# Fused attention and soft mixture of experts: score units of 384 and 2x192 queries, turns in 64-row pieces, another order of tasks

## The chip, the cores and the metric

The kernel runs on one core of one Trainium2 chip. The metric is the device time of one execution in microseconds (us); lower is better. Engines are named as in the profile: PE is TensorE (matmuls), PEld its weight loads, DVE is VectorE, ACT is ScalarE, POOL is GpSimd, SP issues most DMAs.

## The reference: what is computed

The first half is attention over 8 batches of 8 heads, 576 positions by 64 dimensions, in float32. Queries and keys are rotated, the scores are scaled by 1/8, softmax runs over the keys, and the result is multiplied with the values. The second half is a soft mixture of experts over the 4608 tokens of 512 features that come out: logits with 32 slots, a softmax over the tokens (to fill the slots) and one over the slots (to read them back), and between them 8 experts with two layers of weights.

```python
scores = scale * np.matmul(q_rot, k_rot.transpose(0, 1, 3, 2))
scores = scores - np.max(scores, axis=-1, keepdims=True)
attn = np.exp(scores)
attn = attn / (np.sum(attn, axis=-1, keepdims=True) + 1e-09)
return np.matmul(attn, v).astype(np.float32)
```

## The kernel before

Two heads form a pair; there are 32 pairs, and four pairs (one batch) form an image. One head of a pair lies in SBUF rows 0 to 63 and the other in rows 64 to 127. The rotated values are split into a float16 high part and a float16 rest, so a score is a sum of four products: high by high, high by rest, rest by high, and a fourth one that adds the negated maximum (a row of `peak` times a constant in `lift`).

Work on a pair is cut into named tasks:

- `load0/1`, `spin0/1`, `join`, `high0/1`, `low` bring queries and keys in and rotate and split them. `spin` is POOL's, in eight instructions a pair; `join` and `low` are DVE's, `high` is ACT's.
- `m00` to `m31` (`m_unit`, L232 to L237) find the maxima. Four blocks of 128 queries each meet two halves of 288 keys. A unit is two matmuls (one a head, in the two row halves of the array) into a PSUM slot, and one DVE maximum over it. `m_rem` does the last 64 queries; `m_min`, `m_turn`, `m_half`, `m_rows` join the maxima, turn them on PE and send them into `peak`.
- `t0` to `t7` (`t_unit`, L271 to L297) make the exponentials: four key blocks of 128 by two halves of 288 queries. A unit is eight matmuls and one ACT exponential from PSUM into `a_t`. `t8` does the last 64 keys.
- `av0` to `av7` (`av`, L313) multiply with the values: 18 float32 matmuls each, in two column halves of 64. `av8` does the last 64 keys. `av` 2i and 2i+1 use key block i for the two heads.
- `o_out`, `o_down`, `recip`, `norm`, `natural`, `natural_out`, `logits`, `logits_sum` divide by the sum, turn the result (`natural`, five transposes, L367) and form the logits.
- Once an image: `stat`, `slots` and `soft` tasks for the two softmaxes (L393 to L456).

The array is used in several forms of tile, told here as rows by columns: scores and maxima 64x128, the remainders (`t8`, `m_rem`, `av8`) 64x64, `av` 128x64, turns 128x128, `logits` and `slots` 128x32.

All results of matmuls but those of `av` go through three PSUM slots of two banks each, taken in turn (`bank2`, L223); the next use of a slot waits until DVE or ACT has read it.

The order in which each engine meets its tasks is written out by hand: `WHEN` gives each task a due time by pair (modulo 4), `FIRST` that of pairs 0 to 4. The line of all tasks is sorted by due time plus 4 a pair, and each engine, SP and POOL included, works in that order. Tasks of `stat`, `slots` and `soft` do something for every fourth pair only. After the loop follow the last pair, the slots, the two expert layers and the output, with weights that stream in as buffers come free.

Of the kernel before, what the change touches and what calls it, by code (L numbers as in the profile page):

```python
# [7 lines left out]
F32 = mybir.dt.float32  # L8
# [36 lines left out]
N_SLOT = 0  # L45
# [4 lines left out]
N_A = 4  # L50
# [56 lines left out]
    "o_out": (-7.38923, 1.30837, 3.82693, 4.15198, 4.48727), "o_down": (-7.29683, 1.10071, 3.8762, 4.38997, 4.1384),  # L107
    "load1": (-0.7099, -14.46932, -27.91086, -20.43743, -23.33867), "trickle0": 0.4431, "trickle1": 1.2621,
    "trickle2": 2.5296, "trickle3": 3.4658, "recip": (3.8412, 1.95047, 6.75772, 4.80839, 5.05393),
    "high0": (7.26462, -27.61978, -21.33278, -16.62529, -12.03782),  # L110
    "spin1": (7.79554, -28.94545, -24.54925, -20.2484, -19.67269), "norm": (8.00273, 5.36418, 8.13811, 5.60813, 6.09061),
    "load0": (8.7347, -28.06246, -28.81748, -28.24952, -23.67445),
    "natural": (10.20728, 6.24301, 8.6185, 6.45263, 7.72938), "stat0": 10.27075,
    "natural_out": (10.54469, 7.30376, 8.92233, 6.67229, 7.90351),
    "logits": (10.65333, 7.57842, 9.53379, 7.51041, 10.2191),
    "logits_sum": (11.0822, 7.58469, 9.67175, 7.84223, 10.75836), "stat1": 11.4484, "soft0": 11.65971, "soft1": 11.88823,
    "slots": 12.01632, "soft2": 13.55606, "soft3": 14.76066,
    "high1": (19.50237, -27.97373, -20.95698, -15.76925, -12.86183),
    "load_v": (19.88526, -18.22242, -5.34305, -5.07004, -2.7109),
# [5 lines left out]
def attn_softmoe(ctx, tc, qk, v, phi, w, cs, ident, sel, seg, out):  # L125
# [142 lines left out]
    ats = {}  # L268
    rems = {}

    def t_unit(p, u):  # L271
        i, n = divmod(u, 2)
        hl, pk, s = halves[p], peaks[p % 2], bank2()
        for w, (k, q) in enumerate(((KH, QH), (KH, QL), (KL, QH), (None, None))):
            first, last = w == 0, w == 3
            for h in range(2):
                lhs = lift[rows[h]] if k is None else hl[rows[h], k]
                rhs = pk[rows[h]] if k is None else hl[rows[h], q]
                if u < KB - 1:
                    if k is not None:  # L280
                        lhs = lhs[:, P * i:P * i + P]
# [11 lines left out]
        else:  # L293
            if n == 0:
                ats[p, i] = att.tile([P, 2, S], F32, name="a_t", bufs=N_A)
# [614 lines left out]
```

## Time and profile before

| | us |
|---|---|
| median of 3 runs | 532.02 |
| lowest, highest | 531.54, 532.99 |
| span of the profiled execution | 531.8 |
| PE busy | 503.4 (95%) |
| DVE, ACT, POOL busy | 359.4, 309.4, 250.5 |

The profiled execution is one of its own; its span, from the first instruction to the last, is what the stretches below add up to. The page gives busy time by engine, the span in 40 slices, and the groups of instructions by line; the trace answers by stretch and instruction. A matmul's end is modelled, so the distance from one group's start to the next group's start is the better measure of what a group costs PE.

### The profile page before, as it was taken

What the parts mean: (1) busy time and instruction counts of PE and PEld (TensorE: products, weight loads), DVE (VectorE), ACT (ScalarE), POOL (GpSimd) and SP (SyncE); (2) the same over time, 40 slices, a digit from 0 to 9 for tenths busy, and PEclk for the clock granted to TensorE, in tenths of its full rate; (3) what the DMA queues carried; (4) which work ended last, traced back from release to release, by engine and by line L of the source; (5) the groups of instructions that cost most, each with busy time, mean ns of one, the idle gap of its engine ahead of it and who ended that gap; (6) DMA issues with size and microseconds to landing.
All of it is one profiled execution on the core that took longest, in us unless ns stands there. A gap on an engine that the chain in (4) does not pass through costs nothing.

```text
span 531.8 us, 24105 instructions
## 1 busy us (share of the span) xinstructions
PE 503.4 (95%) x10836; PEld 385.8 (73%) x10836; DVE 359.4 (68%) x577; ACT 309.4 (58%) x621; POOL 250.5 (47%) x330
## 2 busy tenths in 40 slices
PE   3799999999999999999999999999999999989991
PEld 2377788878787778787877787778777887853661
DVE  5989867777777777677767776777777762143162
ACT  2156575766675666666666666666666665563352
POOL 3956976636545554655555555555445211210000
PEclk9699999999999999999999999999999999999997
DMA  7244433546441644154425443544345171379998
GB/s 252 95 155 162 162 118 116 197 144 224 140 159 51 215 154 163 48 204 158 161 103 196 157 156 116 193 161 157 116 138 215 38 291 60 134 282 383 394 364 330
DMA packets 28487, 93.92 MB, mean 177 GB/s; under 512 B 4064, under 2 KB 5856, under 8 KB 28384
## 3 DMA queue, kind: packets, MB, share of 16 engines
q1 hardware_dynamic: 28370, 92.37, 48.3%
q8 instruction: 85, 1.39, 1.0%
q14 instruction: 18, 0.15, 0.1%
q10 hardware_dynamic: 14, 0.00, 0.0%
HBM read 82.85 MB, written 9.44 MB: 174 GB/s over the span
## 4 chain that ended last, share of the span: by engine, by line
PE 86%; DVE 6%; ACT 4%; issue 1%; DMA 1%; SPq 0%; DVEq 0%; ACTq 0%
PE o_ps L317 26%; PE s_ps L282 24%; PE s_ps L235 8%; PE o_ps L324 4%; PE s_ps L367 3%; PE a_ps L789 3%; PE a_ps L769 3%; PE s_ps L286 2%; DVE nm L237 2%; PE s_ps L379 2%; PE t_ps L815 2%; PE s_ps L431 1%; PE s_ps L288 1%; PE s_ps L243 1%; DMA x_in<-in_qk 1%
## 5 line engine op out<-in xcount | busy, mean ns | idle before, releaser
L237 DVE TENSOR_REDUCE nm<-s_ps 128x2 f32<-128x576 f32 x256 | 184.9, 754 | 64.0 <-PE s_ps L235 61.9
L200 POOL TENSOR_TENSOR x_in<-x_in,cs_sb 128x288 f32<-128x288 f32 x248 | 197.4, 832 | 55.7 <-DMA x_in<-in_qk 54.2
L297 ACT ACTIVATE a_t<-s_ps 128x576 f32<-128x576 f32 x256 | 150.8, 656 | 117.6 <-PE s_ps L282 116.8
L317 PEld LDWEIGHTS o_ps<-v_in,a_t 128*64 128x64 f32 x4608 | 145.3, 138 | 28.0 <-issue 25.6
L317 PE MATMUL o_ps<-v_in,a_t 128*64 128x65 f32 x4608 | 163.1, 225 | 0.0
L282 PE MATMUL s_ps<-hl 64*128 64x288 f16 x1536 | 135.2, 284 | 0.4 <-DVE nm L237 0.2
L351 POOL TENSOR_TENSOR xn<-o_sb,rr 128x512 f32<-128x512 f32 x31 | 33.4, 1078 | 143.2 <-ACT a_t L297 78.2
L282 PEld LDWEIGHTS <-hl 64*128 64x128 f16 x1536 | 74.6, 94 | 22.8 <-issue 3.0
L282 PE MATMUL s_ps<-peak,lift 64*128 64x288 f16 x512 | 74.9, 283 | 0.0
L235 PE MATMUL s_ps<-hl 64*128 64x288 f16 x512 | 63.6, 290 | 4.9 <-DVE nm L237 2.7
L209 ACT CAST hl<-x_in 128x576 f16<-128x576 f32 (+1 forms) x66 | 41.0, 658 | 17.8 <-DVE x_in L204 17.8
L213 DVE TENSOR_TENSOR hl<-x_in,hl 128x1152 f16<-128x1152 f32 x32 | 45.7, 1429 | 0.5 <-ACT hl L209 0.5
L204 DVE TENSOR_TENSOR x_in<-x_in 128x1152 f32<-128x1152 f32 (+1 forms) x35 | 44.7, 1278 | 0.8 <-POOL x_in L200 0.7
L235 PEld LDWEIGHTS <-hl 64*128 64x128 f16 x512 | 24.7, 96 | 20.1 <-issue 6.6
L245 DVE TENSOR_REDUCE nm<-s_ps 128x2 f32<-128x576 f32 x32 | 24.3, 758 | 16.8 <-PE s_ps L243 16.8
L373 ACT COPY xt<-s_ps 128x576 f32<-128x576 f32 x32 | 20.3, 634 | 17.9 <-PE s_ps L367 17.6
L282 PEld LDWEIGHTS <-lift 64*128 64x128 f16 x512 | 26.6, 94 | 5.5 <-issue 0.5
L324 PE MATMUL o_ps<-v_in,a_rem 64*64 64x65 f32 x1152 | 30.5, 223 | 0.0
L367 PE MATMUL s_ps<-id_sb,xn 128*128 128x128 f32 (+1 forms) x160 | 26.0, 274 | 1.2 <-DVE xn L351 1.2
L324 PEld LDWEIGHTS o_ps<-v_in,a_rem 64*64 64x64 f32 x1152 | 26.4, 133 | 0.5 <-issue 0.2
L297 ACT ACTIVATE a_rem<-s_ps 128x640 f32<-128x640 f32 x32 | 22.6, 705 | 7.0 <-PE s_ps L288 6.6
L367 PEld LDWEIGHTS s_ps<-id_sb,xn 128*128 128x128 f32 (+1 forms) x160 | 19.0, 140 | 7.5 <-issue 7.0
(162 smaller groups left out, 502.0 us busy)
## 6 DMA issues: line engine op xcount, KB each, us to landing
x_in<-in_qk SPq DMA_DIRECT2D x62, 576.0 KB
w_exp<-in_w SPq DMA_DIRECT2D x64, 512.0 KB
v_in<-in_v SPq DMA_DIRECT2D x32, 325.0 KB
out<-w_exp SPq DMA_DIRECT2D x18, 512.0 KB
x_in<-in_qk SPq DMA_DIRECT2D x4, 288.0 KB
cs_sb<-in_cs SPq DMA_DIRECT2D x2, 288.0 KB
peak<-mr SPq DMA_DIRECT2D x31, 2.0 KB
peak<-mr SPq DMA_DIRECT2D x31, 0.2 KB
```

The costliest lines, as they stand in the source:

```text
L200: eng.tensor_tensor(out=x[:, :, c], in0=x[:, :, c], in1=cs_sb[:, :, c], op=ALU.mult)
L204: nc.vector.tensor_tensor(out=x[:, t, 0, c], in0=x[:, t, 0, c], in1=x[:, t, 1, c], op=ALU.add)
L209: nc.scalar.copy(out=halves[p][:, 1 + t, c], in_=loaded[p][:, t, 0, c])
L213: nc.vector.tensor_tensor(out=hl[:, 0:4:3], in0=x[:, :, 0], in1=hl[:, 1:3], op=ALU.subtract)
L235: nc.tensor.matmul(s[:, h, 0:HC], lhsT=hl[rows[h], QH, P * j:P * j + P], rhs=hl[rows[h], KH, half[n]], start=True, stop=True)
L237: nc.vector.tensor_reduce(out=maxima(p)[:, n, j:8:4], in_=s[:, :, 0:HC], axis=AX.X, op=ALU.max, negate=True)
L282: nc.tensor.matmul(s[:, h, 0:HC], lhsT=lhs, rhs=rhs[:, half[n]], start=first, stop=last)
L297: nc.scalar.activation(out=a, in_=s, func=AF.Exp, scale=SCALE)
L317: nc.tensor.matmul(o, lhsT=ats[p, i][:, h, D * t:D * t + D], rhs=vts[p][:, u], start=(i == 0 and j == 0), stop=False)
L324: nc.tensor.matmul(o, lhsT=rems[p][r, at:at + D], rhs=vts[p][r, KB - 1 + h], start=False, stop=(j == (4 if c == h else 3)))
L351: eng.tensor_tensor(out=x[:, 0:4].rearrange("p j h d -> p h j d"), in0=o[:, 1:9, 0:D].rearrange("p (h j) d -> p h j d", h=2), in1=rr[:, 1: ...
L367: nc.tensor.transpose(t[:, P * j:min(P * j + P, S)], xns[p][r, j], id_sb[r, r])
```

## The change

Units. `UNITS` names six units a pair, `x0`, `x1`, `y0`, `x2`, `x3`, `y1`. An x unit takes one 128-row block by 384 columns; a y unit takes two blocks by the remaining 192 columns each. This holds for the maxima (`mx`, `my`: blocks of queries by keys) and for the exponentials (`tx`, `ty`: blocks of keys by queries). Each unit is read by one instruction of 128 x 768 elements in place of 128 x 576. `a_t` becomes two tiles of two key blocks in place of four tiles of one, so `av` 0 to 3 read from `tx0`, `tx1`, `ty0` and `av` 4 to 7 from `tx2`, `tx3`, `ty1`.

Turns. `m_turn`, `natural`, the turns of `slots` and those of `soft` use `turn64`: the 64 upper and the 64 lower rows are transposed apart, each with 64 columns of the identity, into different PSUM banks. `natural` becomes nine pieces in place of five transposes, `m_turn` two in place of one, `stat1` four in place of two, `soft0` three in place of two. What reads them is rearranged to suit.

Order. All due times are new. The last `av` task of a pair in the line, whichever it is, closes the accumulation (`closing`, `ends`).

```diff
-N_SLOT = 0
+N_SLOT = 2
-N_A = 4
+N_A = 2
+XC, YC = 384, 192
+UNITS = ("x0", "x1", "y0", "x2", "x3", "y1")
...
-    def m_unit(p, j, n):
-        hl, s = halves[p], bank2()
-        for h in range(2):
-            nc.tensor.matmul(s[:, h, 0:HC], lhsT=hl[rows[h], QH, P * j:P * j + P], rhs=hl[rows[h], KH, half[n]],
-                             start=True, stop=True)
-        nc.vector.tensor_reduce(out=maxima(p)[:, n, j:8:4], in_=s[:, :, 0:HC], axis=AX.X, op=ALU.max, negate=True)
+    def spans(u):
+        g, k = divmod(u, 3)
+        if k < 2:
+            return g, [(2 * g + k, slice(0, XC), slice(0, XC))]
+        return g, [(2 * g + i, slice(XC, S), slice(YC * i, YC * i + YC)) for i in range(2)]
+
+    def m_unit(p, u):
+        hl, s, (g, ps) = halves[p], bank2(), spans(u)
+        for j, cols, at in ps:
+            for h in range(2):
+                nc.tensor.matmul(s[:, h, at], lhsT=hl[rows[h], QH, P * j:P * j + P], rhs=hl[rows[h], KH, cols],
+                                 start=True, stop=True)
+        o, i, j = maxima(p), s[:, :, 0:XC], ps[0][0]
+        o = o[:, 0, j:8:4] if len(ps) == 1 else o[:, 1, 0:8].rearrange("p (h j) -> p h j", h=2)[:, :, j:j + 2]
+        i = i if len(ps) == 1 else i.rearrange("p h (j x) -> p h j x", j=2)
+        nc.vector.tensor_reduce(out=o, in_=i, axis=AX.X, op=ALU.max, negate=True)
...
+    def turn64(o, i, h):
+        nc.tensor.transpose(o, i[rows[h]], id_sb[rows[h], rows[h]])
+
     def m_turn(p):
         flat[p] = t = bank2()
-        nc.tensor.transpose(t[0:9, 0, 0:P], nms.pop(p), id_sb)
+        nm = nms.pop(p)
+        for h in range(2):
+            turn64(t[0:9, h, 0:D], nm, h)
...
+    PRODUCTS = ((KH, QH), (KH, QL), (KL, QH), (None, None))
+
     def t_unit(p, u):
-        i, n = divmod(u, 2)
+        hl, pk, s, (g, ps) = halves[p], peaks[p % 2], bank2(), spans(u)
+        for w, (k, q) in enumerate(PRODUCTS):
+            for j, cols, at in ps:
+                for h in range(2):
+                    lhs = lift[rows[h]] if k is None else hl[rows[h], k, P * j:P * j + P]
+                    rhs = pk[rows[h], cols] if k is None else hl[rows[h], q, cols]
+                    nc.tensor.matmul(s[:, h, at], lhsT=lhs, rhs=rhs, start=(w == 0 and at.start == 0), stop=(w == 3),
+                                     skip_group_check=True)
+        if (p, g) not in ats:
+            ats[p, g] = att.tile([P, 2, 2, S], F32, name="a_t", bufs=N_A)
...
     def natural(p):
         flat["n", p] = t = bank2().rearrange("p n x -> p (n x)")
         for j in range(NJ):
-            r = slice(0, P) if j < 4 else rows[1]
-            nc.tensor.transpose(t[:, P * j:min(P * j + P, S)], xns[p][r, j], id_sb[r, r])
+            for h in range(j // 4, 2):
+                at = 256 * (h + 1) + D * j
+                turn64(t[:, at:at + D], xns[p][:, j], h)
...
     def slot_tasks(b):
-        nc.tensor.transpose(t[:, 0, 0:P], dt[:, 0:P], id_sb)
-        nc.tensor.transpose(t[:, 0, P:2 * P], dt[:, D:192], id_sb)
+        for c in range(2):
+            for h in range(2):
+                turn64(t[:, h, D * c:D * c + D], dt[:, D * c:D * c + P], h)
...
     def c_soft_tasks(b, tp=None):
-        tp = bank2()[:, 0] if tp is None else tp
+        if tp is None:
+            tp = bank2().rearrange("p n x -> p (n x)")[:, 448:]
+            turn64(tp[:, 0:D], lb[:, 0:P], 0)
+            turn64(tp[:, D:P], lb[:, 0:P], 1)
+            turn64(tp[:, P:P + D], lb[:, D:192], 1)
```

The due times, sorted, give PE this line of tasks for a pair in the steady part (here from `av0` of pair 17 to the next `av0`; the number behind the dot is the pair, and a bar stands where the form of the tiles changes):

```
before: av0.17 av1.17 | m00.19 m21.19 m10.19 | av2.17 av3.17 | t6.17 t7.17 m30.19 | av4.17 av5.17 |
        m_turn.18 natural.16 | m11.19 m20.19 | av6.17 av7.17 | logits.16 | m01.20 t0.18 |
        t8.18 m_rem.19 av8.17 | m31.19 t1.18 t2.18 t3.18 t4.18 t5.18 |
after:  av0.17 av1.17 | m_turn.18 mx1.19 mx0.19 | av5.17 av2.17 av4.17 | mx3.19 natural.15 my1.19 |
        av7.17 av3.17 av6.17 | logits.15 | m_rem.19 t8.18 av8.17 |
        mx2.19 tx1.18 tx0.18 ty0.18 ty1.18 tx2.18 tx3.18 my1.20 |
```

Pairs that close an image have `slots` and `soft` beside it: before, `slots` stands between `m01` and `t0` and the turns of `stat1` and `soft0` beside `m_turn`; after, the line is `logits`, then `stat1`, `tx0`, `soft0` (64x128), then `slots`, then the remainders. Counted over the 32 pairs of the loop, groups of one form follow each other 409 times before and 273 times after: up to `av0.5` 77 and 43, from there to `av0.30` 313 and 211, and behind it 19 and 19. The order of SP, POOL, DVE and ACT is sorted from the same line.

## Rows read from the trace of the kernel before

**Rows 1.** The page, busy time of each engine, share of the span, instructions.

```profile
PE 503.4 (95%) x10836; PEld 385.8 (73%) x10836; DVE 359.4 (68%) x577; ACT 309.4 (58%) x621; POOL 250.5 (47%) x330
```

**Rows 2.** The page, the chain that ended last, shares by engine.

```profile
PE 86%; DVE 6%; ACT 4%; issue 1%; DMA 1%; SPq 0%; DVEq 0%; ACTq 0%
```

**Rows 3.** Stretches: length, busy us by engine, granted clock, DMA share, GB/s.

```profile
28.60:98.80 70.20, 69.21 (x1565) 54.59 (x1563) 56.03 (x76) 43.30 (x80) 49.55 (x56) 1.00 0.43 150
98.80:445.40 346.60, 345.31 (x8056) 274.62 (x8054) 254.85 (x407) 220.65 (x449) 177.44 (x236) 1.00 0.44 153
475.00:531.80 56.80, 45.03 (x494) 25.27 (x494) 19.22 (x34) 22.61 (x47) 1.74 (x2) 0.95 0.94 370
```

**Rows 4.** PE in time order, one pair: start us, length us, line, matmul, count.

```profile
248.53 0.30 PE L235 MATMUL s_ps<-hl 64*128 64x288 f16 x2
...
251.38 1.27 PE L317 MATMUL o_ps<-v_in,a_t 128*64 128x65 f32 x36
252.58 0.54 PE L235 MATMUL s_ps<-hl 64*128 64x288 f16 x6
...
254.25 0.54 PE L282 MATMUL s_ps<-hl 64*128 64x288 f16 x6
...
255.24 0.29 PE L235 MATMUL s_ps<-hl 64*128 64x288 f16 x2
255.46 1.27 PE L317 MATMUL o_ps<-v_in,a_t 128*64 128x65 f32 x36
256.66 0.28 PE L256 MATMUL s_ps<-id_sb,nm 128*9 128x128 f32 x1
...
257.31 0.51 PE L235 MATMUL s_ps<-hl 64*128 64x288 f16 x4
...
258.95 0.43 PE L379 MATMUL s_ps<-xt,phi_sb 128*32 128x128 f32 x8
...
259.50 0.30 PE L235 MATMUL s_ps<-hl 64*128 64x288 f16 x2
...
260.22 0.32 PE L286 MATMUL s_ps<-hl 64*64 64x320 f16 x1
...
261.71 0.29 PE L235 MATMUL s_ps<-hl 64*128 64x288 f16 x2
```

**Rows 5.** PE in time order, the tasks of an image, pair 17 to 18.

```profile
269.84 0.33 PE L419 MATMUL s_ps<-id_sb,d_t 128*128 128x128 f32 x1
...
271.11 0.46 PE L235 MATMUL s_ps<-hl 64*128 64x288 f16 x4
...
272.69 0.43 PE L379 MATMUL s_ps<-xt,phi_sb 128*32 128x128 f32 x8
...
273.16 0.30 PE L235 MATMUL s_ps<-hl 64*128 64x288 f16 x2
273.39 0.42 PE L427 MATMUL s_ps<-xn,dn 64*32 64x128 f32 x8
...
274.75 0.54 PE L282 MATMUL s_ps<-hl 64*128 64x288 f16 x6
```

**Rows 6.** Waits over the whole span: us in total, times, longest.

```profile
PEld o_ps L317 <- issue: 25.6, 108, 0.2
```

**Rows 7.** The chain in order of time: start us, us, what.

```profile
36.16 1.77 PE o_ps L317 x54
```

**Rows 8.** ACT in time order, behind `av8` of the pair of Rows 4.

```profile
249.31 0.21 ACT L341 COPY o_sb<-o_ps 64x65 f32<-64x65 f32 x1
249.54 2.82 ACT L297 ACTIVATE a_t<-s_ps 128x576 f32<-128x576 f32 x5
```

**Rows 9.** DVE in time order, three maxima in a row.

```profile
252.92 2.09 DVE L237 TENSOR_REDUCE nm<-s_ps 128x2 f32<-128x576 f32 x3 [0.63 <-PE s_ps L235]
```

**Rows 10.** Groups by line: busy us, mean ns of one, idle before.

```profile
L317 PEld LDWEIGHTS o_ps<-v_in,a_t 128*64 128x64 f32 x4608 | 145.3, 138 | 28.0 <-issue 25.6
L282 PEld LDWEIGHTS <-hl 64*128 64x128 f16 x1536 | 74.6, 94 | 22.8 <-issue 3.0
```

More of the change, by code (lines that the diff above doesn't have):

```diff
@@ L76 @@
-    "natural": (6.70186, 6.65236, 6.60514, 6.72707), "natural_out": (6.79597, 6.82414, 6.78729, 6.79597),
-    "logits": (7.35988, 7.35988, 7.32871, 7.35629), "logits_sum": (7.55748, 7.56266, 7.52049, 7.57479), "stat0": 8.99027,
-    "stat1": 10.08425, "slots": 11.94902, "soft0": 14.63727, "soft1": 15.70384, "soft2": 16.5487, "soft3": 17.5679,
[8 rows of a table added]
+    "m_min": (-9.24898, -10.07141, -10.65543, -9.67809), "m_turn": (-8.98144, -8.69694, -9.73808, -8.79403),
+    "m_half": (-8.33553, -8.69136, -9.6611, -8.52608), "m_rows": (-7.75001, -7.7324, -7.20975, -8.49008),
[8 rows of a table added]
@@ L79 @@
+    "o_out": (-2.97471, -2.27101, -1.8983, -2.04174), "o_down": (-2.76277, -2.66479, -1.62675, -1.921),
+    "trickle0": 0.4431, "recip": (0.5462, -1.59196, 0.70867, -1.5243), "trickle1": 1.2621,
+    "norm": (1.40693, 2.40265, 2.01973, -0.5723), "weights": (1.52098, 2.94306, 5.30645, 2.79672), "trickle2": 2.5296,
+    "trickle3": 3.4658, "natural": (3.77628, 4.75891, 3.62412, 2.82399),
+    "natural_out": (4.0295, 4.82885, 3.80343, 3.47442), "logits": (4.23692, 5.31816, 4.15935, 3.75073),
[4 rows of a table added]
 }
 FIRST = {
-    "low": (-29.80024, -21.29316, -19.54716, -14.41668, -8.44168),
@@ L108 @@
[L108 to L119, printed above, removed]
+    "soft1": (-106.26016, 16.43236, 10.79557, 11.72811, 7.16191),
@@ new lines @@
+    "my1": (-44.6697, -35.03551, -11.91368, -11.5224, -11.25324),
+    "stat1": (-44.19886, -8.00974, 12.04812, 8.28776, -8.88907),
+    "m_min": (-41.06115, -18.77578, -10.99567, -9.70908, -10.07557),
+    "m_turn": (-39.52861, -15.90387, -8.55189, -9.44574, -9.22444),
+    "m_half": (-29.77836, -15.43198, -8.46718, -8.88665, -8.78896),
+    "m_rows": (-27.94385, -10.69285, -8.32528, -8.59172, -7.86257),
+    "spin0": (-25.18684, -128.90538, -45.55858, -39.20673, -23.3854),
+    "load1": (-24.78219, 0.95005, -3.43378, -39.46747, -25.60339),
@@ new lines @@
+    "tx1": (-24.77367, -7.50828, -6.43911, -7.08093, -5.47045),
+    "t8": (-24.6024, -8.78392, -6.63374, -6.18281, -6.43356),
+    "ty0": (-18.79426, -7.11206, -6.36065, -7.03321, -5.97768),
+    "tx0": (-16.58157, -7.57331, -6.55964, -7.09157, -7.42017),
+    "tx3": (-16.56176, -5.38841, -5.89139, -7.17421, -5.20658),
+    "tx2": (-16.04543, -6.97169, -6.09068, -6.86208, -5.36696),
+    "ty1": (-15.72052, -7.18171, -6.45846, -5.49631, -5.24744),
+    "av0": (-14.0397, -5.03411, -5.63536, -5.11218, -5.0999),
@@ new lines @@
+    "norm": (2.50123, 3.29159, 1.88404, 2.41613, 3.43322), "natural": (2.51048, 3.69668, 3.59742, 2.66055, 3.91089),
+    "trickle2": 2.5296, "natural_out": (3.06016, 4.35405, 3.69233, 3.059, 3.91405),
+    "soft3": (3.24866, 13.93403, -1.18617, 15.43812, -58.85051), "trickle3": 3.4658,
+    "logits": (5.88191, 5.17781, 3.85488, 4.05922, 5.24522),
+    "logits_sum": (6.69807, 5.1858, 4.23867, 4.29405, 5.39864),
+    "high1": (6.80455, -43.55573, -29.59167, -20.40784, -15.69632),
+    "join": (8.39752, -56.14516, -33.18771, -25.40403, -18.6904),
@@ L120 @@
+    "slots": (12.08535, 4.68036, -1.9515, 9.51451, -23.44866),
+    "stat0": (12.87256, -17.45215, -4.13504, 6.88734, 5.35013),
+    "high0": (21.45985, -48.47894, -28.72707, -22.32542, -16.74733),
 }
@@ L269, in attn_softmoe, with t_rem @@
     rems = {}
+    PRODUCTS = ((KH, QH), (KH, QL), (KL, QH), (None, None))
     def t_unit(p, u):
-        i, n = divmod(u, 2)
+        hl, pk, s, (g, ps) = halves[p], peaks[p % 2], bank2(), spans(u)
[8 more added lines that the diff above has]
+            ats[p, g] = att.tile([P, 2, 2, S], F32, name="a_t", bufs=N_A)
+        a, s = ats[p, g], s[:, :, 0:XC]
+        if len(ps) == 1:
+            a = a[:, ps[0][0] % 2, :, 0:XC]
+        else:
+            a, s = a[:, :, :, XC:S].rearrange("p j h x -> p h j x"), s.rearrange("p h (j x) -> p h j x", j=2)
+        nc.scalar.activation(out=a, in_=s, func=AF.Exp, scale=SCALE)
+    def t_rem(p):
         hl, pk, s = halves[p], peaks[p % 2], bank2()
-        for w, (k, q) in enumerate(((KH, QH), (KH, QL), (KL, QH), (None, None))):
+        for w, (k, q) in enumerate(PRODUCTS):
             first, last = w == 0, w == 3
             for h in range(2):
-                lhs = lift[rows[h]] if k is None else hl[rows[h], k]
+                lhs = lift[rows[h], 0:D] if k is None else hl[rows[h], k, 512:S]
                 rhs = pk[rows[h]] if k is None else hl[rows[h], q]
-                if u < KB - 1:
-                    if k is not None:
-                        lhs = lhs[:, P * i:P * i + P]
-                    nc.tensor.matmul(s[:, h, 0:HC], lhsT=lhs, rhs=rhs[:, half[n]], start=first, stop=last)
-                    continue
-                lhs = lhs[:, 0:D] if k is None else lhs[:, 512:S]
                 rhs = rhs.rearrange("p (j x) -> p j x", x=D)
@@ L289, in t_unit @@
                                  skip_group_check=True)
[L290 to L297 removed]
+        rems[p] = a = att.tile([P, 10 * D], F32, name="a_rem", bufs=2)
+        nc.scalar.activation(out=a, in_=s.rearrange("p n x -> p (n x)")[:, 192:832], func=AF.Exp, scale=SCALE)
     o_ps = ps_o.tile([P, 2, 512], F32, name="o_ps")
@@ L311, in cell, with ends @@
         return c, j, o_flat[rows[c], at:at + VC]
+    closing = {}
+    def ends(p, h, c, j, u):
+        return closing[p, h] == u and j == (4 if c == h else 3)
     def av(p, u):
@@ L316, in av @@
             c, j, o = cell(h, t)
-            nc.tensor.matmul(o, lhsT=ats[p, i][:, h, D * t:D * t + D], rhs=vts[p][:, u], start=(i == 0 and j == 0), stop=False)
+            nc.tensor.matmul(o, lhsT=ats[p, i // 2][:, i % 2, h, D * t:D * t + D], rhs=vts[p][:, u], start=(i == 0 and j == 0),
+                             stop=ends(p, h, c, j, u))
     def av_rem(p):
@@ L324, in av_rem @@
                 nc.tensor.matmul(o, lhsT=rems[p][r, at:at + D], rhs=vts[p][r, KB - 1 + h],
-                                 start=False, stop=(j == (4 if c == h else 3)))
+                                 start=False, stop=ends(p, h, c, j, KB - 1))
     def blocks(t):
@@ L597, in attn_softmoe @@
     }
-    for j in range(4):
-        for n in range(2):
-            plan[f"m{j}{n}"] = lambda p, j=j, n=n: m_unit(p, j, n)
+    for u, n in enumerate(UNITS):
+        plan[f"m{n}"] = lambda p, u=u: m_unit(p, u)
+        plan[f"t{n}"] = lambda p, u=u: t_unit(p, u)
+    plan["t8"] = t_rem
     for b in range(KB):
-        plan[f"t{b}"] = lambda p, b=b: t_unit(p, b)
         plan[f"av{b}"] = (lambda p, b=b: av(p, b)) if b < KB - 1 else av_rem
@@ L615, in attn_softmoe @@
     line = sorted((at(name, p), name, p) for name in WHEN for p in range(NPAIR))
+    for _, name, p in line:
+        if name[:2] == "av":
+            u = int(name[2:])
+            closing.update({(p, h): u for h in range(2) if u == KB - 1 or u % 2 == h})
     load(0)
@@ L648, in attn_softmoe @@
             release_io()
-        if held and "wx" in hold and all((f"t{b}", NPAIR - held) in done for b in range(KB)):
+        if held and "wx" in hold and all((f"t{n}", NPAIR - held) in done for n in UNITS + ("8",)):
             held -= 1
```

66 lines of the change are left out of this document (33 added, 33 removed), and 44 rows, old and new, of tables (FIRST, WHEN).

## The prediction

> **What bounds the kernel now.** I read the page's busy times first. TensorE is busy for 95% of the span and no other engine for more than 68% [rows 1]. Then the chain of waits: 86% of what sets the end is PE, 1% DMA [rows 2]. Then the stretches. From 28.6 us to 475 us PE has hardly a gap (345.3 of 346.6 us in the long stretch) at a granted clock of 1.00, with DMA at 0.44 [rows 3]; only the end, 475 to 531.8, is full of DMA (0.94), and no line of it belongs to this change. So the question is what PE spends inside one pair. The 25 pairs between 98.8 and 445.4 take 346.60 / 25 = 13.86 us each [rows 3].
>
> A pair without image work runs from 248.53 to 261.71, 13.18 us [rows 4]. From start to start, in us: scores and maxima 2.85 (248.53 to 251.38), 0.47 (252.58 to 254.25 less an `av` group of 1.20), 1.21 (254.25 to 255.46), 0.44 (257.31 to 258.95 less 1.20), 0.72 (259.50 to 260.22), together 5.69; four `av` groups of 1.20 each, 4.80; the turns 0.65 (256.66 to 257.31); logits 0.55; remainders 1.49.
>
> Two prices are hidden in these. Sixteen score matmuls of 288 columns take 0.99 us (254.25 to 255.24), two side by side, so 0.124 a couple; the next couple, the last before an `av` group, takes 0.22 (255.24 to 255.46). Leaving the score form thus costs 0.10; three couples in 0.47 say the same (0.37 + 0.10). An `av` group of 36 takes 1.20 and one of 54 takes 1.77 [rows 7], so 18 matmuls are 0.57 and a group has 0.05 on top. The waits confirm it: 108 times the first weight load behind a score group stood idle for some 0.24 us with nothing to release it [rows 6]. Forty couples stream in 40 x 0.124 = 4.96; with five exits (0.50) that is 5.46 of the 5.69, and 0.23 are waits, most of it in the run of five `t` units, which is 2.85 instead of 21 x 0.124 + 0.10 = 2.70.
>
> **The change part by part, a pair without image work.**
>
> *Columns.* Four x units of 384 and two y units of 2 x 192 are 2304 columns, as eight of 288 were, in as many matmuls. The stream stays at 4.96. [...]
>
> *Order.* The sorted line has three score groups a pair in place of five: exits 0.30 for 0.50. `av` goes as 36 + 54 + 54: 1.20 + 1.77 + 1.77 = 4.74 for 4.80. The remainders follow `logits` directly and stay at 1.49. `logits` waits for nothing late, so it takes the 0.47 that it takes in the image pair (272.69 to 273.16) [rows 5] in place of 0.55.
>
> *Turns.* Five transposes and one of the maxima make 0.65 now, a group of their own. No row shows a 64-row piece. Bounds: a turn of 128 columns takes about 0.11 (0.65 for five full ones, a last one of 64, and the way out); a piece has 64 columns, so 0.055. If the two halves run side by side, as the two matmuls of every score couple do, six couples are 0.33; if they follow each other, eleven pieces are 0.60. Both ends are saved the group of their own. I take 0.33, since score couples are the same form of tile.
>
> *Waits.* All six `t` units now stand in one run between maxima, so each meets ACT. Five exponentials of 576 follow each other every (2.82 - 0.65) / 4 = 0.54 us, 0.65 being the length of one [rows 8]; 768 elements are at most 0.72 in proportion. PE makes a `t` unit in 4 x 0.165 = 0.66. ACT is free about 1.0 after the score group began (249.54 against 248.53), then ends exponential k at 1.0 + 0.72 k. PE, with a maximum of 0.17 in front, starts unit k + 1 at 0.17 + 0.66 k. Three slots and the maximum make unit 4 wait for exponential 1 (1.72 against 2.15), 5 for 2 (2.44 against 2.81), 6 for 3 (3.16 against 3.47), and the closing maximum for 4 (3.88 against 4.13). ACT gives way each time, by 0.25 at the least. What is late next is that closing maximum, if a cast stands in ACT's queue inside the run; in the sorted line `high0` and `high1` stand behind it. DVE: three maxima in 2.09 are 0.67 apart [rows 9], so at most 0.89 for 768; six of these replace eight of 0.67, 5.3 for 5.4 a pair, no relief and no new load. The last exponential is done at 5.3, when PE ends `av0`, `av1` (4.30 + 0.10 + 1.20 = 5.6); the next maxima take its slot. So the 0.23 of waits goes; because I followed only one pair's queues, I put 0.10 back.
>
> *Sum.* 4.96 + 0.30 + 0.33 + 4.74 + 0.47 + 1.49 = 12.29 for 13.18: 0.89 saved, 0.79 with the 0.10.
>
> *Image work.* It adds (13.86 - 13.18) x 4 = 2.7 an image. Two turns beside `m_turn` make that group 1.27 (269.84 to 271.11) for 0.65; `slots` costs 0.23 + 1.36 (273.16 to 274.75) and splits a score group; `soft` turns do the rest [rows 5]. After: 1.36, one exit of 0.10, four couples of pieces at 0.055, and 0.2 of what I can't place: 1.9. Saved 0.8 an image, 0.20 a pair.
>
> *Whole.* 25 pairs x (0.79 + 0.20) = 24.8. Before 98.8 the groups fall from 77 to 43: 34 x 0.075 (the mean of 0.10 and 0.05) = 2.5, and seven turn groups gain 1; PE is full there from 28.6 on [rows 3], so this counts, while the first 28.6 us hang on DVE's maxima, whose sum is unchanged. Say 3, between 0 and 6, for I can't follow all first waits of POOL and SP. The pairs behind 445.4 keep 19 groups, but their turns get shorter: 1. Together 28.8: 531.8 - 28.8 = 503.0. The median of the runs lies 0.2 above this span, which I leave out. SP's and POOL's queues pass loads and `norm` in another order; POOL is busy 47% and hides this, and one pair's chain of load, `spin` and `join` would have to be late by more than the 0.25 above to be seen.
>
> [...]
>
> **The rivals.**
>
> 1. *The weight load paces short couples.* A load of 64x128 float16 lasts 94 ns, one of float32 138 [rows 10]. If a half of the array held each load that long, the 20 couples of 192 (16 in `ty`, 4 in `my`) would cost 0.011 more each, and six turn couples 0.083 more: 0.72 a pair, x 32 = 23, so 526. Against: `av` starts two matmuls every 0.064 (1.15 / 18) with loads of 138, so a load's length is mostly latency.
> 2. *The same mechanism, slower than before.* If the two halves' loads also follow each other, a couple of 192 takes 0.188, 0.105 more: 20 x 0.105 = 2.1 a pair, 67 in all: 503 + 67 = 570. It decides for slower from 0.045 a couple on (0.89 / 20), that is, from 0.128. For it: no score couple here is shorter than 0.124. Against: the quadrants of the remainders start six loads and matmuls within 0.13 (260.22 on), and `av` as above.
> 3. *Turn pieces follow each other.* 0.60 for 0.33, 0.27 a pair, 9 in all, with the images 1.5: 513. For: the pieces are float32 where scores are float16. Against: `av` is float32 and runs two halves at once.
> 4. *The run of `t` is ACT's.* If casts (0.67 each) or a late `o_out` fall into it, each pair gives back 0.3 to 0.6: 512 to 522. For: ACT waits 0.25 at the least, so one cast is too much. Against: the sorted line.
> 5. *No waits at all*, and a start 6 shorter: 531.8 - 25 x 1.09 - 6 - 1 = 497.5.
>
> **How the numbers follow.** The forecast 0.60 (own range 499 to 508), rival 1 0.06, rival 2 0.05, rival 3 0.12, rival 4 0.08, rival 5 0.09. About 0.3% is what can be told from no change here. Faster: all but rival 2 and a tail of rivals 1 and 4, 0.93; the same 0.02; slower 0.05. The range 495 to 517 leaves out rivals 1 and 2 and half of 4, and the far end of 5.
>
> **What would show it.** A pair of 12.2 to 12.5 us in the long stretch; 18 matmuls of `av` unchanged; a couple of 192 columns about 0.083 apart; the pieces of `natural` done in 0.3; a run of six `t` units with a closing maximum of about 4.4 before `av0`. I am wrong if couples of 192 columns start 0.10 or more apart, if the turn pieces take 0.11 a couple, or if score matmuls wait for ACT.

## The result and the profile after

| | before | after |
|---|---|---|
| runs of one session, us | 530.74 to 532.99 | 514.2, 517.05, 522.35, 522.6 |
| span of the profiled execution | 531.8 | 515.3 |
| ratio of times, 95% interval | 1 | 0.9696 [0.9656, 0.9736] |

The ratio leaves out the two runs of 522, which lie over 1.5% above the fastest. 0.9696 x 531.8 is 515.6, where 503 was forecast: the change is worth 16.2 us, and the sum gave 28.8. A second measurement of the same kernel gave 517.14 (514.07 to 522.58, six runs), 0.9724 [0.969, 0.9758]. From its lowest to its highest run the new kernel scatters by 1.6%, the old one by 0.6%.

The page after: busy time by engine, the granted clock in 40 slices, PE's instruction queue (packets, MB, share), the chain that ended last.

```profile
PE 479.7 (93%) x11017; PEld 380.3 (74%) x11017; DVE 360.9 (70%) x513; ACT 298.1 (58%) x557; POOL 272.5 (53%) x330
...
PEclk9679998999999999999999999999999989989996
...
q8 instruction: 86, 1.41, 1.1%
...
PE 83%; DMA 5%; DVE 4%; POOL 2%; issue 2%; ACT 2%; SPq 1%; ACTq 0%; DVEq 0%; POOLq 0%
```

PE's busy time fell by 23.7 us, more than the span did (16.5): PE has idle time that it did not have [rows 1]. In the chain, DMA has 5% for 1% and issue 2% for 1% [rows 2]. The stretches tell where (columns as in [rows 3]; 100.70 is the first `av` of pair 5, which stood at 98.75 before, and 427.10 that of pair 30, before 445.4):

```profile
0.00:28.60 28.60, 15.33 (x95) 8.09 (x96) 22.25 (x32) 5.53 (x10) 18.52 (x27) 0.77 0.63 215
28.60:100.70 72.10, 68.82 (x1599) 55.67 (x1599) 52.79 (x63) 42.79 (x70) 48.04 (x56) 0.95 0.34 113
100.70:427.10 326.40, 321.49 (x8157) 267.33 (x8155) 257.55 (x355) 209.47 (x390) 197.85 (x235) 0.99 0.47 164
427.10:459.00 31.90, 28.89 (x678) 23.81 (x676) 9.08 (x30) 17.55 (x43) 6.34 (x12) 0.95 0.47 166
```

In this profile the loop gained 20.3 us (346.7 to 326.4) and everything else lost: the start 2.0, and what lies behind `av0` of pair 30 takes 88.2 for 86.4. (A second profile, shown below, agrees on the loop and the end, but not on the start.) Even in the loop PE stands idle for 4.9 us, where it was 1.3 before.

One pair without image work, PE in time order (columns as in [rows 4]):

```profile
257.33 1.27 PE L362 MATMUL o_ps<-v_in,a_t 128*64 128x65 f32 x36
258.53 0.22 PE L283 MATMUL s_ps<-id_sb,nm 64*9 64x64 f32 x2
258.59 0.49 PE L260 MATMUL s_ps<-hl 64*128 64x384 f16 x4
259.01 1.85 PE L362 MATMUL o_ps<-v_in,a_t 128*64 128x65 f32 x54
260.80 0.34 PE L260 MATMUL s_ps<-hl 64*128 64x384 f16 x2
260.97 0.41 PE L283 MATMUL s_ps<-id_sb,xn 64*128 64x64 f32 x8
261.21 0.22 PE L283 MATMUL s_ps<-id_sb,xn 64*128 64x64 f32 x1
...
265.26 0.34 PE L260 MATMUL s_ps<-hl 64*128 64x384 f16 x2
265.44 0.65 PE L313 MATMUL s_ps<-hl 64*128 64x384 f16 x6
...
266.74 0.66 PE L313 MATMUL s_ps<-hl 64*128 64x192 f16 x12
267.39 0.66 PE L313 MATMUL s_ps<-hl 64*128 64x192 f16 x12
...
269.36 0.33 PE L260 MATMUL s_ps<-hl 64*128 64x192 f16 x4
269.61 0.28 PE L362 MATMUL o_ps<-v_in,a_t 128*64 128x65 f32 x2
```

The pair takes 12.28 us (257.33 to 269.61); 12.29 was the sum. Two turns of maxima take 0.06 (258.53 to 258.59), the nine pieces of `natural` 0.30 (260.97 to about 261.27), the six `t` units 3.92 (265.44 to 269.36), and a y unit's eight couples of 192 columns 0.65 (266.74 to 267.39), 0.082 each. So the kernel's parts cost what the sum said. The rest of this document is about what the sum did not hold.

Where PE stood idle, from the view of waits (engine, what it waited to write, releaser: us in all, times, longest):

```profile
PE s_ps L332 <- DMA peak<-mr: 3.6, 2, 2.5
PE o_ps L362 <- issue: 2.6, 3, 1.6
PE s_ps L260 <- DVE nm L265: 2.4, 4, 1.0
PE s_ps L313 <- issue: 2.3, 3, 1.2
PE s_ps L283 <- issue: 1.9, 1, 1.9
PE s_ps L283 <- DVE xn L397: 1.4, 1, 1.4
...
PE s_ps L427 <- ACT xt L420: 0.8, 1, 0.8
```

Four of these in time order (in brackets the idle time before and its releaser):

```profile
22.44 0.28 PE L283 MATMUL s_ps<-id_sb,nm 64*9 64x64 f32 x2 [1.93 <-issue]
...
29.09 0.42 PE L332 MATMUL s_ps<-peak,lift 64*64 64x320 f16 x1 [1.13 <-DMA peak<-mr]
...
164.06 0.51 PE L313 MATMUL s_ps<-hl 64*128 64x192 f16 x8 [1.20 <-issue]
...
420.37 0.32 PE L332 MATMUL s_ps<-peak,lift 64*64 64x320 f16 x1 [2.48 <-DMA peak<-mr]
```

The row at 164.06 is the odd one: PE stops in the middle of one `t` unit, between matmuls that wait for nothing but PE. There are six such places, at 73.8 (1.61), 96.2 (0.36), 162.9 (1.20), 169.6 (0.39), 249.8 (0.61) and 438.5 us (0.78). PE's instructions come by DMA in blocks: 86 in q8 for 1.41 MB, so 16 KB each, and 22034 matmuls and loads over 86 are 256 a block. I counted, at the landing of each block, the instructions of PE begun so far (matmuls, loads and 99 semaphore waits) less 256 for each block landed earlier. This lead is 299 in the median, and its six highest values (449, 447, 435, 427, 410, 404) fall on those six places; at no instant of any run is it above 449. Before, the median is 283 and only one lead is over 400 (419 at 435.5, with no gap of 0.3 us beside it). The six stalls say the same more sharply. They come after 2241, 3265, 6593, 6849, 10945 and 20417 instructions, each of them 193 more than a multiple of 256; PE has then begun 449 more than the landed blocks hold, and it goes on 1.2 to 1.5 us after the next block has landed. In the thirteen profiles other than that of the kernel before, every wait of PE of 0.28 us or more without a releaser stands at such a count, except the one at the first turn of maxima. So PE had, by these counts, six times run out of instructions. At six of the 86 blocks it stood for 0.36 us or more; why those six came late is what the experiments put to the test.

The other waits have names, or causes that other rows show. At 22.44 the first turn of maxima waits, since DVE took `join` of pair 1 ahead of the last two maxima and itself waited for POOL (DVE in time order):

```profile
16.48 0.94 DVE L265 TENSOR_REDUCE nm<-s_ps 128x2 f32<-128x768 f32 x1
18.47 1.93 DVE L222 TENSOR_TENSOR x_in<-x_in 128x1152 f32<-128x1152 f32 x1 [1.05 <-POOL x_in L218]
20.32 1.81 DVE L265 TENSOR_REDUCE nm<-s_ps 128x2 f32<-128x768 f32 x2
22.17 0.17 DVE L277 TENSOR_REDUCE nm<-nm 128x9 f32<-128x18 f32 x1
```

At 29.09 and 420.37 the small transfer of the maxima is late: the second was issued at 413.56 and 414.13, behind eight weight loads of 512 KB issued from 401.5 to 412.8. Near the end `logits` of pair 30 waits 0.78 at 447.7 and `natural` of pair 31 1.43 at 449.0 (1.20 before). The granted clock is at half (0.50) for 17.1 us in the start (15.6 to 32.6; before for 10.2, 17.5 to 27.7), and for 3.4 us each from 77.0, 421.8 and 452.5, a few us after waits of 1.61, 2.48 and 1.43.

### The profile page after: what moved, and what is told of

The parts are those of the page before. It is cut to its first block, busy times and chain, and to the rows that moved or that the text cites. A ratio compares the mean times of both kernels' runs of the same rounds, so it can differ in the third digit from the quotient of the medians.

```text
span 515.3 us, 24311 instructions
## 1 busy us (share of the span) xinstructions
PE 479.7 (93%) x11017; PEld 380.3 (74%) x11017; DVE 360.9 (70%) x513; ACT 298.1 (58%) x557; POOL 272.5 (53%) x330
## 3 DMA queue, kind: packets, MB, share of 16 engines
q1 hardware_dynamic: 28370, 92.37, 50.2%
q8 instruction: 86, 1.41, 1.1%
## 4 chain that ended last, share of the span: by engine, by line
PE 83%; DMA 5%; DVE 4%; POOL 2%; issue 2%; ACT 2%; SPq 1%; ACTq 0%; DVEq 0%; POOLq 0%
PE o_ps L362 27%; PE s_ps L313 22%; PE s_ps L260 7%; PE o_ps L370 4%; PE s_ps L283 3%; PE a_ps L849 3%; PE a_ps L829 3%; DMA x_in<-in_qk 3%; POOL x_in L218 2%; DMA peak<-mr 2%; PE s_ps L427 2%; PE t_ps L875 2%; PE s_ps L332 2%; PE s_ps L271 1%; PE s_ps L481 1%
## 5 line engine op out<-in xcount | busy, mean ns | idle before, releaser
L218 POOL TENSOR_TENSOR x_in<-x_in,cs_sb 128x288 f32<-128x288 f32 x248 | 204.7, 861 | 124.6 <-DMA x_in<-in_qk 109.2
L265 DVE TENSOR_REDUCE nm<-s_ps 128x4 f32<-128x768 f32 (+1 forms) x192 | 177.3, 953 | 52.1 <-PE s_ps L260 51.0
L322 ACT ACTIVATE a_t<-s_ps 128x768 f32<-128x768 f32 x192 | 140.1, 824 | 16.8 <-PE s_ps L313 15.0
L313 PE MATMUL s_ps<-hl 64*128 64x384 f16 (+1 forms) x1536 | 129.6, 288 | 2.7 <-issue 2.3
L313 PE MATMUL s_ps<-peak,lift 64*128 64x192 f16 (+1 forms) x512 | 65.0, 287 | 0.0
L397 POOL TENSOR_TENSOR xn<-o_sb,rr 128x512 f32<-128x512 f32 x31 | 38.0, 1225 | 43.1 <-DVE rr L393 24.6
L260 PE MATMUL s_ps<-hl 64*128 64x192 f16 (+1 forms) x512 | 57.0, 291 | 3.3 <-DVE nm L265 2.4
L273 DVE TENSOR_REDUCE nm<-s_ps 128x2 f32<-128x576 f32 x32 | 23.9, 746 | 4.5 <-PE s_ps L271 4.5
L439 DVE TENSOR_TENSOR l_sb<-s_ps,l_sb 128x192 f32<-128x192 f32 x24 | 8.6, 358 | 24.3 <-PE s_ps L430 24.3
L405 POOL TENSOR_TENSOR xn<-o_sb,rr 64x128 f32<-64x128 f32 x31 | 23.3, 750 | 2.4
```

What stands on the lines that cost most here:

```text
L218: eng.tensor_tensor(out=x[:, :, c], in0=x[:, :, c], in1=cs_sb[:, :, c], op=ALU.mult)
L260: nc.tensor.matmul(s[:, h, at], lhsT=hl[rows[h], QH, P * j:P * j + P], rhs=hl[rows[h], KH, cols], start=True, stop=True)
L265: nc.vector.tensor_reduce(out=o, in_=i, axis=AX.X, op=ALU.max, negate=True)
L273: nc.vector.tensor_reduce(out=maxima(p)[:, :, 8], in_=s[:, :, 0:HC], axis=AX.X, op=ALU.max, negate=True)
L313: nc.tensor.matmul(s[:, h, at], lhsT=lhs, rhs=rhs, start=(w == 0 and at.start == 0), stop=(w == 3), skip_group_check=True)
L322: nc.scalar.activation(out=a, in_=s, func=AF.Exp, scale=SCALE)
```

## The experiments

Ratios are to the kernel before on the same chip, with a 95% interval.

**The same again.**

> The changed kernel once more, for its spread and a second profile. Theory (late instruction blocks): PE's stalls in the middle of a task, 5 to 7 us in the first profile, come back, but at other places, because they depend on which transfer a 16 KB block of PE's instructions meets; times between 513 and 523. Rival (a wait in the order of the tasks): the same stalls at the same tasks, spread as small as before's (0.5%).

0.9724, as told. The profile spans 512.4: `av0` of pair 5 comes at 96.46, the loop takes 327.3, the rest 88.7. So loop and end are as in the first profile, but the start, which was 2.0 us later than in the kernel before, is 2.3 earlier here. The named waits came back at the same places (2.58 at 19.7, 1.04 at 27.8, 2.29 at 414.9, 1.42 at 445.9). Of the six stalls inside tasks three came back, at the same instructions: 159.3 (0.95), 245.9 (0.38) and 435.2 (0.91), after 6593, 10945 and 20417, with leads 443, 400 and 431.

```profile
160.26 0.50 PE L313 MATMUL s_ps<-hl 64*128 64x192 f16 x8 [0.95 <-issue]
```

This is the place that stood at 164.06 in the first profile. The other three are gone or under 0.3 us. So neither theory nor rival held as told: which blocks are late follows the order of tasks in part, since the transfers beside them do too, and how late they are changes from run to run (5.0 us of such waits in the first profile, 2.2 here).

**More traffic.**

```diff
 nc.sync.dma_start(out=vts[p], in_=v[p])
+nc.sync.dma_start(out=dram.tile([P, 10, VC], F32, name="v_more", bufs=2), in_=v[p])
```

> The changed kernel with one more transfer of 325 KB a pair that nothing reads: v is also copied into a scratch in DRAM, behind its load on SP's queue. Theory (late instruction blocks behind data): more stalls of PE in the middle of tasks, 3 to 15 us slower than the changed kernel, so 519 to 531. Rival (waits in the order of tasks, data is early anyway): within 2 us of the changed kernel.

533.53 (529.26 to 536.79), 1.0026 [1.0, 1.0053]: 16 us over the run before it, the whole gain, and above the 519 to 531 of the theory. Waits, and one place in PE's order of time:

```profile
PE o_ps L363 <- issue: 7.4, 5, 2.2
...
PE s_ps L333 <- DMA peak<-mr: 4.9, 2, 3.8
PE s_ps L261 <- DVE nm L266: 4.6, 8, 1.0
```

```profile
156.16 1.61 PE L363 MATMUL o_ps<-v_in,a_t 128*64 128x65 f32 x44
160.00 0.56 PE L363 MATMUL o_ps<-v_in,a_t 128*64 128x65 f32 x10 [2.23 <-issue]
```

An `av` group stops after 44 of its 54 matmuls for 2.23 us. Leads of 432 or more come eight times, and the dry places add up to 12.2 us. But the extra bytes make other transfers late too (3.8 for the maxima of pair 30), so the 16 us are not the blocks' alone.

**Less traffic, by the values.**

```diff
+if p >= 2:
+    vts[p] = vts[p - 2]
+    return
```

> The changed kernel with the loads of v left out from pair 2 on (the values of pairs 0 and 1 are used again, so the output is not the reference's). Theory: 325 KB less a pair, fewer late instruction blocks, 3 to 7 us faster than the changed kernel, so 509 to 513, and a smaller spread. Rival: no PE wait names a load of v, so within 2 us of the changed kernel.

514.33 (513.07 to 517.99), 0.9684 [0.9658, 0.971]; stalls of 0.91, 0.65 and 2.31 stayed. 2.8 us under the same kernel with its values, with overlapping intervals: this settled nothing.

**A longer warm-up.**

```diff
-N_HEAT = 12
+N_HEAT = 20
```

> The changed kernel with 20 spare matmuls ahead of the first turn of maxima in place of 12; they fill a stretch of 1.9 us in which PE stood idle and waited for DVE. Theory (the start lost time to the half clock, 15.6 to 32.6 us in the profile): the full clock is back some 5 us sooner and 2 to 3 us are saved, 512 to 515. Rival (the start is DVE's): the clock comes back sooner or not, the time stays within 1 us of the changed kernel.

520.1, 0.9752 [0.9718, 0.9785]: nothing gained. The turn's wait shrank to 0.86 as PE was busy beside it, the turn itself came at 22.25 for 22.29 in the second profile of the changed kernel, and the wait for the transfer grew to 1.76. The full clock was back at 34.0, not sooner (31.7 in that second profile). By these rows the start hangs on DVE and on transfers. Why its clock is at half for longer than before (17.1 and 13.7 us in the two profiles, for 10.2) remains open.

**The old turns in the new kernel.**

```diff
-turn64(t[:, at:at + D], xns[p][:, j], h)
+nc.tensor.transpose(t[:, P * j:min(P * j + P, S)], xns[p][r, j], id_sb[r, r])
```

(the same in `m_turn`, `slots` and `soft`)

> The changed kernel with the turns of before (whole 128-row transposes in m_turn, natural, slots and soft); units and order stay new. Theory of the prediction: a pair pays 0.32 for the longer turns and up to 0.25 more for leaving the score form twice, 0.4 to 0.6 a pair, so the long stretch has pairs of 12.7 to 12.9 us instead of 12.28 and the time is 13 to 20 us above the changed kernel (516.5), 529 to 537. Rival (order and units do it all, pieces gain nothing): pairs of 12.3 to 12.4, within 3 us of 516.5.

531.86 (527.35 to 535.25), 0.9997 [0.9966, 1.0028]. PE in time order, a pair without image work:

```profile
263.16 1.27 PE L360 MATMUL o_ps<-v_in,a_t 128*64 128x65 f32 x36
264.36 0.28 PE L287 MATMUL s_ps<-id_sb,nm 128*9 128x128 f32 x1
264.57 0.50 PE L260 MATMUL s_ps<-hl 64*128 64x384 f16 x4
...
267.05 0.86 PE L411 MATMUL s_ps<-id_sb,xn 128*128 128x128 f32 x5
267.64 0.43 PE L260 MATMUL s_ps<-hl 64*128 64x192 f16 x4
...
276.09 0.33 PE L360 MATMUL o_ps<-v_in,a_t 128*64 128x65 f32 x3
```

The pair takes 12.93: the turn of the maxima stands alone between forms and costs 0.21 for 0.06, `natural` 0.59 for 0.30. The time is inside what was expected, the pair 0.03 above it. A plain pair is still 0.25 shorter than before the change, and the loop takes 344.1 for 346.7, but the start and the end give it back (99.5 for 98.75, 89.8 for 86.4): in the time, the new order and units without the pieces gain nothing.

**The pieces alone in the old kernel.**

> The kernel before with the 64-row pieces alone; units and order stay old. Theory: the turns' group of 0.65 becomes about 0.33 inside a score group, pairs of 12.8 to 12.9 instead of 13.18, so 518 to 523. Rival (the pieces need the new order to be worth anything): above 528.

(Only the `turn64` parts of the change, with what reads them.) 527.14, 0.9913 [0.9887, 0.9938]; 518 to 523 was expected. One pair in four does fall to 12.82, by 0.36, but an image pair stays at 15.26, and of the other two one falls by 0.15 and one by nothing:

```profile
268.22 0.48 PE L255 MATMUL s_ps<-id_sb,xn 64*128 64x64 f32 x9
...
269.26 0.46 PE L235 MATMUL s_ps<-hl 64*128 64x288 f16 x4 [0.56 <-ACT dn L432]
```

In the image pair the turns are over sooner, and the maxima behind them wait for ACT to read the slot that they need (seven times, 3.4 us in all). The old order spent that time on turns.

**Eight units of 288 in the new order.**

(In the code two units of 128 x 576 stand for each y unit and one for each x unit; due times are unchanged.)

> The changed kernel with eight units of 288 in place of six of 384 and 2 x 192, in the new order (each y task does two units); turns stay new. Theory (columns are the same, a unit's size only gives ACT room in the run of exponentials): 8 x 0.53 on ACT against 8 x 0.495 on PE leaves waits of 0.1 to 0.4 a pair at the end of the run, so 519 to 529. Rival 1 (the units are the gain): pairs of 12.8 or more, above 532. Rival 2 (units are worth nothing): within 2 us of 516.5.

558.99 (557.29 to 559.29), 1.05 [1.0474, 1.0526], far outside what my theory allowed (519 to 529); rival 1 said above 532. PE's waits:

```profile
PE s_ps L260 <- DVE nm L262: 11.3, 26, 0.6
PE s_ps L280 <- DVE nm L262: 7.0, 12, 0.7
...
PE s_ps L260 <- ACT a_t L314: 5.1, 21, 0.2
PE s_ps L260 <- ACT xt L412: 3.8, 7, 0.5
```

With eight units a pair goes round the three slots oftener, and PE waits more for slots to be read: 18.3 us for maxima on DVE and 5.1 for exponentials on ACT, although ACT itself takes little longer (4.45 us for eight exponentials, 4.33 for six of 768). Pairs without image work take 13.74 to 14.74. I had called the units neutral; in this order, which was made for six, they are what makes it work.

**The named waits mended.**

```diff
+("join", 1): -41.0, ("high0", 1): -40.9,             # behind the first maxima
+# recip and norm of 30 earlier; natural, logits of 29 and 30 earlier
-eng.dma_start(out=pk[0:65:64, 512:S], in_=mr[8:9])
+nc.sync.dma_start(out=pk[0:65:64, 512:S], in_=mr[8:9])
-if "wx" not in hold and ("low", NPAIR - 1) in done:
+if "wx" not in hold and ("low", NPAIR - 1) in done and ("m_rows", NPAIR - 2) in done:
```

> The changed kernel with its order mended in three places where the profile shows PE waiting for something named: join of pair 1 behind the maxima of pair 0, and the second small transfer of its maxima on SP ahead of the next loads; the last weights released behind the transfer of the maxima of pair 30; the turns and logits of pairs 29 and 30 before the end of av of pair 31. Theory (these waits and the half-clock stretches behind them are what the forecast missed): 2 to 4 us at the start, 2.5 to 4 before the end of the loop, 2 to 4 at the end, so 505 to 510. Rival (late instruction blocks are the rest and take the place of the waits): 512 or more.

512.3 (511.34 to 516.13), 0.9642 [0.9591, 0.9693], and measured again:

> e7_mended once more beside it, for a comparison on one chip: 511 to 514; its stalls in the middle of tasks again some 5 to 7 us.

514.79 (511.99 to 518.01), 0.9687 [0.9653, 0.9721]. The rival's number came true (512 or more), not the 505 to 510. Of the three mends one is plain in both profiles: the wait of 2.48 at pair 30 is gone, and the way from `av0` of pair 29 to that of pair 30 takes 13.5 us, where it took 16.5 and 16.2. `av0` of pair 5 comes at 96.98 and 97.96, where the kernel as changed had 100.70 and 96.46: that shows no gain, and PE now waits 2.1 and 1.8 us for a cast of ACT where it waited for `join`. The end takes 86.6 and 88.0 for 88.2 and 88.7. The clock is full from 29.9 to 504 and from 29.5 to 507. But the loop is no shorter (327.7 and 329.3 for 326.4 and 327.3), because PE runs dry more: 1.08, 1.17, 0.66, 0.62, 0.38, 1.14, 1.05, 1.11 and 0.82, 8.0 us, and 9.6 in the second profile, for 5.0 and 2.2 in the kernel as changed. The intervals overlap with those of the kernel as changed (0.9696, 0.9724): better by some 0.5%, not surely.

**The two loads of a pair apart.**

```diff
+if name == "load1" and p >= 2 * NP:
+    return at("m_rows", p - 3) + 0.0001
```

> e7_mended with the two 576 KB loads of a pair (from pair 8 on) parted on SP: the second stands behind the transfer of the maxima of the pair in work, some 3 us later. Theory (a block of PE's instructions is late when it meets a long run of data; e7_mended still lost some 7 us to it): shorter runs of data, fewer late blocks, 2 to 4 us faster than e7_mended (512.3), 508 to 510. Rival (the amount of data counts, not its grouping): within 1 us of e7_mended.

535.32 (531.41 to 538.38), 1.0062 [1.0036, 1.0088]: 20 us slower than the mended order, which neither theory nor rival allowed. Waits:

```profile
PE s_ps L260 <- DVE nm L265: 19.0, 19, 2.2
```

The second load came later, `spin` and `join` behind it, and PE waited 19 times for maxima. The load was moved by some 3 us, so the chain of load, `spin` and `join` has less than that to spare, and POOL does not hide a later load. On the blocks it says little, as PE was slower.

**Little traffic.** (The code is shortened; the values of pairs from 4 on are likewise those of two pairs before.)

```diff
+loaded[p] = kept[p] = kept[p - 2] if p >= 4 else io.tile(...)
+nc.sync.dma_start(out=loaded[p][0:16, t], in_=qk[p, t, 0:16])  # from pair 4 on
```

> The mended order, with little traffic in the loop: from pair 4 on a load of queries or keys brings 16 of the 128 rows and works on the tile of two pairs ago, and the values are those of pairs 2 and 3; the tables of the rotation are set to one at pair 4. The transfers of a pair fall from 1477 KB to 144 KB, and no instruction of PE changes. Theory (PE's instruction blocks come late because they share the transfer engines with the loads): between 98 and 415 us PE waits nowhere for more than 0.3 us in a task, no lead there is above 400 instructions, and the time is 505 to 509 us. Rival (the blocks are late by PE's own pace of 43 instructions a us, whatever else moves): the stalls of about 5 us in the loop stay, and the time is 511 to 515.

504.84 (503.76 to 507.62), 0.9469 [0.9449, 0.9488], just under the theory's 505 to 509, lower than the mended order by 1.7 to 2.2% of the time before and apart from both its intervals. (This kernel leaves most of its data out, so what it computes is not the attention.) The same stretch of the loop, first in the mended order, then here:

```profile
98.00:415.00 317.00, 311.00 (x7922) 259.98 (x7917) 255.26 (x343) 203.07 (x380) 204.37 (x232) 1.00 0.47 157
```

```profile
98.00:415.00 317.00, 316.17 (x8107) 264.91 (x8107) 252.51 (x352) 206.95 (x386) 190.02 (x234) 1.00 0.20 65
```

PE is idle for 0.8 us of 317 in place of 6.0 and gets through 185 more matmuls, which took 7.4 us in the mended order. From `av0` of pair 5 to that of pair 30:

```profile
96.32:415.66 319.34, 318.51 (x8155) 266.42 (x8153) 253.53 (x353) 209.29 (x390) 190.65 (x234) 1.00 0.20 66
```

This is 8.4 and 10.0 us less than the mended order took. One stall over 0.3 us is left in the loop (0.55 at 157.9, lead 415), where I had allowed none and no lead above 400; the median lead falls from 305 to 273. At 427, when the weights stream in, PE still runs dry for 2.46 us with a lead of 449. Instructions of PE and their order are the same, and it runs faster, so its own pace is not what makes the blocks late: the other transfers are. Some 5 us of the loop's gain are dry places. What else the lighter traffic relieves, the other 3 to 5, I did not trace.

**The values later.**

```diff
+if name == "load_v" and p > NP:
+    return 4 * p - 7.15
```

> The mended order with one due time moved: the values of a pair are asked for behind its maxima's transfer (4p - 7.15 for -8 to -10), so that they no longer follow the loads of queries and keys at once. Same bytes. Theory (a pile of transfers makes the blocks late, and spreading it helps): the dry stalls in the loop fall from about 5 us to 2, time 508 to 511. Rival (what counts is the sum of the bytes, or a load of 576 KB is enough by itself): the stalls stay, 512 to 516. A third: the values come too late for av0 and PE waits for them, over 520.

516.97 (513.58 to 517.37), 0.9685 [0.9656, 0.9714]. The rival held, 1 us above its range: stalls of 1.36, 0.66, 0.53 and 1.89 in the loop, and, of the third, one wait of 2.8 for values at 425. Asking for a fifth of the bytes later does not help.

## Why the prediction was right and wrong

**Right: the prices.** The plain pair (12.28 for 12.29), pieces side by side (0.30, with the maxima's 0.36, where 0.33 was put and rival 3 had 0.60), couples of 192 at 0.082, the unchanged `av` (1.20 and 1.78), `logits` 0.47. Images add 1.75 where 1.9 was put. Rivals 1 to 3 fell with these rows: couples of 192 go every 0.082 and couples of turn pieces every 0.06, with loads that last 96 and 138 ns. Rival 4 fell too: no `t` unit in the loop waits for ACT.

**Luck: the range.** The time lies inside 495 to 517, but 12 us above the forecast and outside the 499 to 508 that the forecast itself was given. The range reached up there for rivals 3 and 4, which fell; what held the time up was in none of the rivals.

**Wrong: the step *Whole*.** It multiplied an undisturbed pair by 25 and took the start and the end as short sums of PE's own work. Against its parts, in the first profile and the second (spans 515.3 and 512.4, 12.3 and 9.4 above the 503.0):

- *Start*, forecast 3 saved: 2.0 lost and 2.3 saved, so 5.0 and 0.7 off. The named waits (1.93 and 1.13, 2.58 and 1.04) stand in both, so they do not make the difference. The first profile alone has dry places of 1.61 and 0.36 there, and 3.4 us of half clock behind the longer one, which cost about 1.7 by my estimate (half of 3.4): together 3.7 of the 4.2 between the two. "Whose sum is unchanged" was true of DVE's maxima, but what stands between them changed (`join` of pair 1 ahead of the last two); that moving it gains anything is not shown.
- *Loop*, 4.5 and 5.5 off. At the prices that the rows show it would take 25 x 12.28 + 6.25 x 1.75 = 317.9, and with little traffic it took 319.3; it took 326.4 and 327.3. Of the first profile's 8.5, the late transfer at pair 30 is 2.48, the half clock behind it about 1.7 by the same estimate, dry places 2.2; some 2 are small waits that I leave open (some 4 in the second). The waits that I put back (0.10 a pair) and the images' smaller price covered about 4 of it.
- *End*, 2.8 and 3.3 off: 1.8 and 2.3 lost for 1 saved. The last pair's `recip` and `norm` stood behind `logits_sum` of pair 30, the clock fell again (to 0.50 for 3.4 us in the first profile), and 0.78 and 0.91 were dry.
- "POOL is busy 47% and hides this" was wrong in the start (DVE waited 1.05 for POOL with the maxima queued behind). In the loop POOL would not have hidden a load that comes 3 us later, as the loads set apart show.

**Wrong as a step, though not in the sum: the units as neutral, the turns and the order as separate terms.** I priced columns, turns and waits one by one. The pieces alone gave 0.9%, the rest without them nothing, both together 3.0%; the order without the bigger units lost 5%. So the new order needs the pieces and the bigger units; the bigger units in the old order were not run. The new order puts the six `t` units into one run; that the three slots carry six reads there and not eight is argued from the waits for slots, not shown apart from the maxima's.

**Not in the prediction at all: instructions as a resource.** It put this term at nothing. A shorter pair asks for the same blocks in less time (in the loop 50 matmuls and loads a us for 46.5), beside as many bytes of other transfers (92.37 MB in q1, before and after). The waits are 4.95 us of the 12.3 missing in the first profile (the six places) and 2.2 of the 9.4 in the second; the half clock behind one of them adds to the first.

## What to carry to other kernels

When PE is made faster, list what must reach it per pair besides data: its own instructions too. Here they came in blocks of 16 KB beside the loads: between 98 and 415 us of the mended order PE was idle for 6.0 us with 1477 KB of loads a pair, and for 0.8 with 144 KB. The mark of it was a wait inside one task with no releaser (0.36 to 1.61 us in the first profile); count instructions begun against blocks landed, see whether such waits stand at one number of each block, and test by taking bytes away. Take a second profile before you explain a stretch: the start here was 2.0 us slower than before in one and 2.3 faster in the other. And price the first and the last pair by following each engine's queue there, as the waits of a steady pair say nothing of them.

## What the runs showed of the hardware

- PE ran dry when 449 of its instructions had begun beyond the blocks landed, always after the same number of each 256 (193), and went on 1.2 to 1.5 us after the next landing (six of six in the changed kernel). The lead never passed 449 in any run. At the landings its median is 288 to 308 in the new order with 1477 KB a pair, and 273 with 144 KB.
- Two transposes of 64 float32 rows run side by side in the two row halves: 0.06 us a couple in `natural`, although the weight load of each lasts 138 ns in the records; score couples of 192 columns go every 0.082 with loads of 96.
- A single turn in the 128x128 form between two other forms costs 0.21 us; two pieces in the form around them cost 0.06.
